# Value products with exchanged operands in 21 units of a fused attention and feed-forward kernel

## The chip, the cores and the metric

The kernel runs on one core of a Trainium2 chip. A core has engines that work side by side, each through its own instructions in order: TensorE (PE; PEld are its weight loads), VectorE (DVE), ScalarE (ACT), GpSimd (POOL) and SyncE (SP, which here only issues transfers). SBUF is the working memory, PSUM the one in which TensorE leaves its products; both have 128 partitions. The metric is the device time of one execution in microseconds (us). TensorE's clock can be throttled; the profile has a row for what was granted.

## The reference

Two parts, one behind the other, computed here in bf16 operands with f32 sums. `P` is an 8x8 matrix per head that mixes the 8 blocks of 96 tokens.

```python
B, H, S, D = 4, 8, 768, 64            # 8 blocks of 96 tokens
P = sinkhorn(sort_net)                # five rounds of exp and normalising, per head 8x8
k_sorted, v_sorted = P @ k_blocks, P @ v_blocks
scores = q_block @ k_sorted_block.T / sqrt(D)          # 96x96 per head and block
attn = exp(scores - max(scores)); attn = attn / (sum(attn) + 1e-9)
x = attn @ v_sorted_block             # then (tokens, heads*64): 3072 x 512
h = x @ w_in                          # 512 x 2048
out = (h * cos(h)) @ w_out            # 2048 x 512
```

## The kernel before

The 3072 tokens are cut into 8 chunks `n` of 384 tokens, half a batch each, and a chunk into four units `u` of one block of 96 tokens with all 8 heads (4 pairs `h2` of two, `hp`). A chunk's attention is followed by its feed-forward layer, and while one chunk's layer runs the next chunk's attention is fed in between. The order is written out by hand: `PLAN` (L18 on) is a list of some 800 steps, and each step issues its instructions to the engines' queues in that order. An engine does its instructions strictly in this order, so a step that waits holds up everything behind it on the same engine.

The steps that matter here, for unit `n u`:

- S or T: scores on TensorE. M (L1362) and X (L1376, L1372): VectorE takes the maximum per row and subtracts it. E (L1380): ScalarE's exponential gives the weights, in bf16, query by row.
- TP (L1407) and TE, or TD (a transposing transfer): the weights turned to `pT`, 96 key rows by 8 heads x 96 queries.
- AV (L1431): eight products on TensorE, one per head, with `pT` as the stationary operand and the mixed values (64 columns and a column of ones) as the moving one. The output has the queries in its partitions, and 65 columns per head: 64 sums and, in the last, the sum of the weights.
- N (L1447, L1448): VectorE takes the reciprocal of the 8 sums per query and multiplies the 512 sums with them, into `xn` in bf16.
- XP (L1470) and XE (L1071 on ScalarE, L1073 on VectorE): four turns of `xn` on TensorE, into PSUM, and a copy to `xT`, the layer's input with features in its partitions. In 11 of the 32 units a transposing transfer (XD) does both; these units are not touched by the change. In chunks 0 to 2 the token order inside a unit is permuted (queries are loaded four rows at a time), and the turns set it right by multiplying with a permuted identity, `order` (L1154).
- U (L1500), C (L1506) and G (L1512): the layer's first product, its cosine on ScalarE and the multiply on VectorE; U4 (L1523), C4, G4 (L1536) are the same for chunk 0, by halves of 192 tokens, so that its first half needs units 0 and 1 alone. D (L1545), O and W: the second product, the copy out of PSUM and the store.
- QP and QE turn later queries and copy them; k and v mixing (kp, ks, kg, v0, vb, vg and their copies, kse and vbe among them) run in between.

PSUM is shared out as three tiles of two banks (`big`, "B" in the plan) and two of one bank (`acc`, "c"). AV, U, U4 and most scores use `big`: a tile comes free when its last reader is done, and the third next `big` step waits for it. In chunk 0 AV is preceded by a few idle products (`keep_warm`).

Of the kernel before, what the change touches and what calls it, by code (L numbers as in the profile page):

```python
# [65 lines left out]
kxp 0  # L66
TP 0 1 c
X 0 2
AV 0 0
z_turned 1  # L70
TE 0 1 V
E 0 2 0
TP 0 3 c
Lk 1
Lv 1
N 0 0
AV 0 1
N 0 1
pk2
TE 0 3 A  # L80
TP 0 2 B
TE 0 2 A
QP 1 1 c
QE 1 1 0 V
XP 0 0 B
XE 0 0 A
XP 0 1 c
z_vperm
XE 0 1 V
AV 0 2  # L90
N 0 2
AV 0 3
z_turned 0
U4 0 0 0
U4 0 0 1
C4 0 0
p_pads
N 0 3
U4 0 1 0
QE 1 1 1 V  # L100
XP 0 3 c
G4 0 0
U4 0 1 1
C4 0 1
XP 0 2 c
XE 0 2 V
U4 0 3 0
U4 0 3 1
G4 0 1
XE 0 3 A  # L110
U4 1 2 0
U4 1 3 0
C4 0 3
# [57 lines left out]
TP 1 3 c  # L171
TE 1 3 A
TP 1 0 B
AV 1 2
X 1 1
W 0 1
TE 1 0 A
W 0 0
D 0 2 1
D 0 2 2  # L180
AV 1 3
E 1 1 1
TP 1 1 c
AV 1 0
TE 1 1 A
N 1 2
XP 1 2 B
XE 1 2 A
N 1 3
D 0 2 3  # L190
AV 1 1
O 0 2 t A
W 0 2
ks 3 B
kse 3 A
N 1 0
XP 1 0 B
XE 1 0 A
ks 2 c
kse 2 A  # L200
N 1 1
XP 1 3 c
XE 1 3 V
ks 1 B
XP 1 1 B
XE 1 1 V
# [97 lines left out]
D 1 1 0  # L304
D 1 1 1
D 1 1 2
AV 2 0
Lpv 3 6
Lpv 4 6
Lpv 5 6  # L310
N 2 0
kg 4 c
kge 4 A
Lq 4
# [2 lines left out]
E 2 3 2  # L317
D 1 1 3
M 3 0
AV 2 1  # L320
N 2 1
kg 3 B
O 1 1 o A
X 3 0
D 1 2 0
kge 3 A
TP 2 3 c
AV 2 2
N 2 2
XP 2 1 B  # L330
XE 2 1 V
D 1 2 1
TE 2 3 A
AV 2 3
kg 5 B
N 2 3
XP 2 2 B
XP 2 0 c
E 3 0 0
D 1 2 2  # L340
XP 2 3 B
XE 2 2 V
W 1 1
XE 2 3 A
D 1 2 3
XE 2 0 V
kge 5 A
U 2 0
C 2 0
# [77 lines left out]
D 2 1 1  # L427
M 4 0
X 4 0
AV 3 1  # L430
N 3 1
vge 0 8 A
D 2 2 0
E 4 0 1
D 2 1 2
D 2 1 3
AV 3 2
vg 4 8 B
AV 3 3
N 3 3  # L440
D 2 2 1
D 2 2 2
S 4 1 c 0
N 3 2
XP 3 1 B
vge 4 8 A
XE 3 1 V
XP 3 3 B
vg 6 8 B
XE 3 3 V  # L450
O 2 1 o A
vge 6 8 A
XP 3 2 B
XE 3 2 V
D 2 2 3
O 2 2 o V
W 2 1
# [87 lines left out]
TD 5 0  # L545
E 5 1 0
TD 5 1
AV 4 2
N 4 2
D 3 2 0  # L550
AV 4 3
D 3 2 1
D 3 2 2
XP 4 2 B
QD 6
N 4 3
XP 4 3 B
hq 0
XE 4 2 A
D 3 2 3  # L560
Lq 7
XE 4 3 V
U 4 1 1
C 4 1
O 3 2 v V
# [63 lines left out]
XD 5 2  # L629
D 4 1 3  # L630
O 4 1 v A
AV 5 3
D 4 2 0
N 5 3
D 4 2 1
XP 5 3 B
XE 5 3 A
E 6 1 1
D 4 2 2
D 4 2 3  # L640
# [66 lines left out]
E 7 0 1  # L707
D 5 1 3
O 5 1 v A
AV 6 3  # L710
N 6 3
TD 7 0
T 7 2 B
D 5 2 1
# [1 line left out]
X 7 1  # L716
E 7 1 2
TD 7 1
XP 6 3 B
XE 6 3 A  # L720
W 5 0
M 7 2
D 5 2 2
# [48 lines left out]
D 6 1 0  # L772
D 6 1 1
D 6 1 2
AV 7 2
D 6 1 3
O 6 1 v V
D 6 2 0
AV 7 3
N 7 2  # L780
N 7 3
D 6 2 1
XP 7 2 B
D 6 2 2
XD 7 1
XP 7 3 B
D 6 2 3
XE 7 3 A
XE 7 2 V
U 7 0  # L790
W 6 0
W 6 1
# [40 lines left out]
def kernel(  # L833
# [36 lines left out]
    const = ctx.enter_context(tc.tile_pool(name="const", bufs=1))  # L870
# [18 lines left out]
    ident = const.tile([128, 128], BF16, name="ident")  # L889
# [19 lines left out]
    vS = {}  # L909
    QR, NQ = 4, 3  # L910
# [115 lines left out]
    def picks(t, batches):  # L1026
        nc.gpsimd.memset(t[:], 0.0)
        for z, b in enumerate(batches):
            picked(t, z, b)
# [5 lines left out]
        nc.gpsimd.memset(vS[g][:, :, D:D + 1], 1.0)  # L1035

    picks(pick, (1, 0, 1))
    order = const.tile([blk, blk], BF16, name="order")
    warm = const.tile([128, 128], BF16, name="warm")
    nc.vector.memset(warm[:], 0.0)  # L1040
    half_pi = const.tile([128, 1], FP32, name="half_pi")
    nc.vector.memset(half_pi[:], math.pi / 2)
    nc.vector.memset(vperm[:, CD:], 0.0)
    nc.vector.memset(kbuf[:64, :32 * D], 0.0)
    nc.vector.memset(q_turned[0][:, :, QW:], 0.0)
# [21 lines left out]
    V, A = nc.vector, nc.scalar  # L1067
# [31 lines left out]
    E, Q = E_eps[:, :, :nb], Q_eps[:, :nb]  # L1099
# [209 lines left out]
    s_t, pT, xn_t, xT, gt, out_ps, kept = {}, {}, {}, {}, {}, {}, {}  # L1309
# [102 lines left out]
    def v_at(g, b2, hp, h2, i):  # L1412
        return (b2 * 2 + hp) * NB + h2 * nb + i

    def AV(n, u, pool=big, tag="big"):
# [11 lines left out]
        for hp in range(2):  # L1427
            for h2 in range(H2):
# [5 lines left out]
                    vS[g][:, v_at(g, b2, hp, h2, ih * IC + u), :D + 1],  # L1434
                    start=True, stop=True)

    def N(n, u):
        r = small.tile([blk, 2, H2], FP32, name="r", tag="r")
        xn = xn_t[n, u] = small.tile([blk, H2, 2, D], BF16, name="xn", tag="xn")
        parts = [slice(0, 2)] if ("a", n, u) in ps else [slice(0, 1), slice(1, 2)]  # L1440
        for e in parts:
            if len(parts) == 1:
                a = ps.pop(("a", n, u))[:blk, :, :H2 * (D + 1)]
            else:
                a = ps.pop(("a", n, u, e.start))[:blk, :H2 * (D + 1)].unsqueeze(1)
            avv = a.rearrange("p e (h w) -> p e h w", w=D + 1)
            nc.vector.reciprocal(r[:, e].unsqueeze(3), avv[:, :, :, D:])  # L1447
            nc.vector.tensor_tensor(  # L1448
                xn.rearrange("p h e d -> p e h d")[:, e], avv[:, :, :, :D],
                r[:, e].to_broadcast([blk, e.stop - e.start, H2, D]), op=ALU.mult)  # L1450
# [11 lines left out]
    def XP(n, u, pool, tag, to=None):  # L1462
        us = range(u, (u if to is None else to) + 1)
        o = kept_tile(("x", n, u), pool, tag, [128, KC, len(us), blk], BF16, "xps")

        turn = order[:] if n < NQ else ident[:blk, :blk]
        for i, z in enumerate(us):
            xn = xn_t.pop((n, z))
            for h2 in range(H2):
                nc.tensor.transpose(  # L1470
                    o[:, h2, i], xn[:, h2].rearrange("p e d -> p (e d)"), turn)
# [204 lines left out]
```

## Time and profile before

| what | value |
|---|---|
| median of three timed runs | 235.09 us (235.08 to 235.13) |
| span of the profiled execution | 233.6 us |
| instructions | 5709 |
| AV on TensorE | 32 units of 8 products, 193 ns each from issue to end |
| N on VectorE | 32 reciprocals of 198 ns, 32 multiplies of 687 ns |
| XP on TensorE | 84 turns, 205 ns each from issue to end |
| XE | 12 copies on VectorE of 348 ns, 9 on ScalarE of 475 ns |

The profile is of one execution, taken by the hardware profiler. The profiled execution has no timed figure of its own beside its span; the span runs from its first to its last instruction and lies 1.5 us under the timed median. Busy time is what an engine's instructions cover. Products on TensorE are pipelined: the duration of one product is longer than the distance to the next, so the cost of a group is read from the chain of work, which shows distances, and not from durations. A row of the timeline gives the start, the length, the engine, the line, the operation with output and input, and how many instructions it merges; what stands in brackets is the engine's idle time before it, and what ended it. A row of the groups by line gives busy time and mean duration behind the bar, and then the idle time ahead of the group.

### The profile page before, as it was taken

How to read it: one execution, taken by the hardware profiler on the slowest of the kernel's cores; microseconds unless marked ns; L12 is line 12 of the kernel's file. 1: busy time of each engine (PE TensorE's matmuls, PEld its weight loads, DVE VectorE, ACT ScalarE, POOL GpSimd, SP SyncE). 2: the span in 40 equal slices, each digit the busy share in tenths (PEclk: the TensorE clock that was granted, in tenths of full speed). 3: DMA queues.
4: the chain of work that ended last, by engine and by line, in shares of the span. 5: the costliest groups of instructions: out<-in, count | busy, mean ns of one | idle time of the engine just before them, and what ended most of it. 6: DMA issues, size and time to landing. Idle time of an engine off the chain costs nothing.

```text
span 233.6 us, 5709 instructions
## 1 busy us (share of the span) xinstructions
PE 224.9 (96%) x2358; PEld 148.6 (64%) x2378; DVE 173.8 (74%) x290; ACT 149.9 (64%) x199; POOL 93.7 (40%) x117
## 2 busy tenths in 40 slices
PE   8799999999999999989999999999999999999994
PEld 5379899567665666645666558645655596456553
DVE  5759986897889777886778977898587779445630
ACT  3367965668869768783789746764766376536411
POOL 7689996598970186963508001700000000000000
PEclk9999999999999999999999999999999999999999
DMA  5999999994899899997989659954943360250103
GB/s 74 222 194 206 205 207 227 198 209 144 105 108 156 186 163 157 101 208 144 137 161 81 90 94 167 196 85 78 149 157 68 66 189 3 50 141 3 46 0 135
DMA packets 66842, 31.01 MB, mean 133 GB/s; under 512 B 55553, under 2 KB 62337, under 8 KB 66561
## 3 DMA queue, kind: packets, MB, share of 16 engines
q0 software_dynamic: 24048, 13.64, 42.8%
q1 hardware_dynamic: 42480, 16.83, 34.3%
q8 instruction: 18, 0.29, 0.5%
q10 hardware_dynamic: 288, 0.20, 0.3%
q14 instruction: 8, 0.06, 0.1%
HBM read 27.27 MB, written 6.29 MB: 144 GB/s over the span
## 4 chain that ended last, share of the span: by engine, by line
PE 77%; DMA 7%; ACT 4%; POOL 4%; DVE 3%; issue 2%; SPq 1%; POOLq 0%; ACTq 0%
PE o L1545 28%; PE h L1500 27%; PE h L1523 5%; DMA kv<-in_v_dram 3%; PE av L1431 3%; POOL vperm L993 2%; DMA kTs<-kTs 2%; PE vs L1258 2%; PE sc L1321 2%; PE o L1640 2%; DMA pT<-p_buf 1%; PE pps L1407 1%; PE vs L1293 1%; PE xps L1470 1%; PE ks L1202 1%
## 5 line engine op out<-in xcount | busy, mean ns | idle before, releaser
L1545 PE MATMUL o<-w_out_t,gg 128*128 128x512 bf16 x349 | 85.1, 379 | 1.1 <-issue 0.2
L1500 PE MATMUL h<-xT,w_in_t 128*128 128x384 bf16 (+1 forms) x524 | 78.4, 303 | 0.0
L1512 DVE TENSOR_TENSOR gg<-c,h 128x768 bf16<-128x768 f32 x56 | 52.8, 948 | 21.2 <-ACT c L1506 21.1
L1506 ACT ACTIVATE c<-h,half_pi 128x768 f32<-128x768 f32 x56 | 50.4, 901 | 20.0 <-PE h L1500 18.8
L1500 PEld LDWEIGHTS <-w_in_t 128*128 128x128 bf16 x524 | 47.7, 98 | 22.2 <-DVE xT L1073 0.4
L1545 PEld LDWEIGHTS <-gg 128*128 128x128 bf16 x368 | 33.1, 98 | 32.9 <-DVE gg L1512 0.6
L1380 ACT ACTIVATE p_buf<-s 96x768 bf16<-96x768 f32 x32 | 26.4, 841 | 12.7 <-DVE s L1376 10.3
L1362 DVE TENSOR_REDUCE mx<-sc 96x8 f32<-96x768 f32 (+1 forms) x41 | 31.5, 771 | 0.7 <-PE sc L1321 0.4
L993 POOL COPY vperm<-kv 64x1536 bf16<-64x1536 bf16 (+1 forms) x10 | 28.1, 2848 | 3.7 <-DMA kv<-in_v_dram 3.7
L1376 DVE TENSOR_TENSOR s<-sc,mx 96x384 f32<-96x384 f32 (+1 forms) x33 | 24.2, 733 | 1.3
L1448 DVE TENSOR_TENSOR xn<-av,r 96x512 bf16<-96x512 f32 x32 | 22.0, 687 | 1.1
L943 POOL DMA_DIRECT2D kv<-in_q_dram x24 | 16.0, 680 | 0.8 <-issue 0.5
L1071 ACT CAST kTs<-ks 128x512 bf16<-128x512 f32 (+1 forms) x18 | 11.0, 635 | 3.6 <-PE ks L1202 3.6
L943 POOL DMA_DIRECT2D q_mem<-in_q_dram x16 | 10.7, 684 | 3.4 <-DMA kv<-in_v_dram 2.9
L1447 DVE RECIPROCAL r<-av 96x8 f32<-96x8 f32 x32 | 6.3, 198 | 7.3 <-PE av L1431 7.1
L1523 PE MATMUL h<-xT,w_in_t 128*128 128x192 bf16 x128 | 11.4, 246 | 0.0
L1060 PE MATMUL idle<-warm 128*128 128x512 bf16 (+4 forms) x46 | 9.0, 364 | 2.3 <-ACT q_turned L1143 1.2
L1060 PEld LDWEIGHTS <-warm 128*128 128x128 bf16 x106 | 7.7, 111 | 5.5 <-issue 2.8
L1071 ACT COPY kv<-o 128x512 f32<-128x512 f32 (+2 forms) x10 | 5.3, 528 | 9.1 <-PE o L1545 6.5
L1071 ACT COPY xT<-xps 128x384 bf16<-128x384 bf16 x9 | 4.3, 475 | 10.3 <-PE xps L1470 10.3
L1523 PEld LDWEIGHTS <-w_in_t 128*128 128x128 bf16 x128 | 10.4, 98 | 0.1
L1568 POOL CAST held<-q_turned 96x1 f32<-96x1 bf16 x2 | 0.4, 182 | 24.4 <-DVE gg L1512 16.9
(120 smaller groups left out, 276.5 us busy)
## 6 DMA issues: line engine op xcount, KB each, us to landing
out_dram<-kv SPq DMA_DIRECT2D x12, 256.0 KB, 2.4
out_dram<-o_s SPq DMA_DIRECT2D x10, 256.0 KB, 3.0
w_in_t<-in_moe_w_in_dram POOLq DMA_DIRECT2D x4, 512.0 KB, 12.4
w_out_t<-in_moe_w_out_dram POOLq DMA_DIRECT2D x4, 512.0 KB, 12.7
kv<-in_k_dram POOLq DMA_DIRECT2D x2, 768.0 KB, 10.2
kv<-in_v_dram POOLq DMA_DIRECT2D x2, 768.0 KB, 13.6
pair<-in_k_dram POOLq DMA_DIRECT2D x2, 768.0 KB, 10.9
kv<-in_v_dram POOLq DMA_DIRECT2D x6, 256.0 KB, 6.1
```

The source lines that it names most:

```text
L943: nc.gpsimd.dma_start(out=q_heads[:, i, :, e], in_=src[:, ih * IC + i, :, e])
L993: nc.gpsimd.tensor_copy(dst, src)
L1071: eng.copy(dst, src)
L1362: nc.vector.reduce_max(mx[:], s_view(n, u, hp), axis=AX.XY if n < 2 else AX.X)
L1376: nc.vector.tensor_tensor(s, sc, mx.to_broadcast(list(s.shape)), op=ALU.subtract)
L1380: nc.scalar.activation(p[:, :, :blk], s_t.pop((n, u)).rearrange("p e h c -> p (e h) c"), AF.Exp, scale=scale)
L1448: nc.vector.tensor_tensor(xn.rearrange("p h e d -> p e h d")[:, e], avv[:, :, :, :D], r[:, e].to_broadcast([blk, e.stop - e.start, H2, D]) ...
L1500: nc.tensor.matmul(o[:, f2, x * w:(x + 1) * w], w_in_t[:, kk, f * 128:(f + 1) * 128], xT[n][:, kk, x * w:(x + 1) * w], start=(kk == 0), st ...
L1506: nc.scalar.activation(c[:], ps["h", n, fp][:, :, :TC], AF.Sin, bias=half_pi[:, 0:1])
L1512: nc.vector.tensor_tensor(gt[n, fp // 2][:, f:f + 2], ps.pop(("c", n, fp))[:], ps.pop(("h", n, fp))[:, :, :TC], op=ALU.mult)
L1523: nc.tensor.matmul(o[:, part, f2 * w:(f2 + 1) * w], w_in_t[:, kk, f * 128:(f + 1) * 128], xT[0][:, kk, h * w:(h + 1) * w], start=(kk == 0) ...
L1545: nc.tensor.matmul(out_ps[n, ts][:], gt[n, q][:, f % 4, ts * 128:(ts + 1) * 128], w_out_t[:, f, :], start=(f == 0), stop=(f == FC - 1))
```

## The change

In 21 units the steps AV, N, XP and XE are replaced by two, AT and NT. The 21 are all units of chunks 0, 1 and 2, units 1 to 3 of chunk 3, units 2 and 3 of chunks 4 and 7, and unit 3 of chunks 5 and 6. In the plan AT and NT stand where AV and N stood; XP and XE go.

AT exchanges the operands of the value products: the mixed values (64 columns) are stationary and the turned weights move, 96 columns per head. Heads with `e` = 0 fill output partitions 0 to 63, those with `e` = 1 partitions 64 to 127, so the output is `xT` before its normalisation. The sums come out of two products of a block of ones (`unit`, 96x64) with 4 heads x 96 columns of weights each; every output partition of a half holds the sum that belongs to its column. NT takes the reciprocal of all these 128x384 sums, writes it as f32 over the unit's `pT`, and multiplies the 128x384 products with it, straight into `xT`. In chunks 0 to 2 the multiply's access pattern sets the token order right, and `order` goes.

```diff
@@ the plan, chunks 1 and 7 as examples @@
-AV 1 0
+AT 1 0
 TE 1 1 A
-N 1 2
-XP 1 2 B
-XE 1 2 A
-N 1 3
+NT 1 2
+NT 1 3
 D 0 2 3
...
-AV 7 3
-N 7 2
-N 7 3
+AT 7 3
+NT 7 2
+NT 7 3
 D 6 2 1
-XP 7 2 B
 D 6 2 2
 XD 7 1
-XP 7 3 B
 D 6 2 3
-XE 7 3 A
-XE 7 2 V
 U 7 0
...
@@ the start @@
-    order = const.tile([blk, blk], BF16, name="order")
...
+    unit = const.tile([blk, D], BF16, name="unit")
+    nc.vector.memset(unit[:], 1.0)
...
-            A.copy(
-                order.rearrange("k (p r) -> k p r", r=QR),
-                ident[:blk, :blk].rearrange("k (r p) -> k p r", r=QR))
...
@@ the new steps @@
+    def AT(n, u, pool=big, tag="big"):
+        g, b2, ih = where(n)
+        a = kept_tile(("at", n, u), pool, tag, [128, 2, 512], FP32, "at")
+        pt = pT[n, u].rearrange("p a c -> p (a c)")
+        if n == 0:
+            keep_warm(1, a[:, 1], 256)
+        for h2 in range(H2):
+            for e in range(2):
+                x = (e * H2 + h2) * blk
+                nc.tensor.matmul(
+                    a[e * D:(e + 1) * D, 0, h2 * blk:(h2 + 1) * blk],
+                    vS[g][:, v_at(g, b2, e, h2, ih * IC + u), :D], pt[:blk, x:x + blk],
+                    start=True, stop=True)
+        for e in range(2):
+            nc.tensor.matmul(
+                a[e * D:(e + 1) * D, 1, :H2 * blk], unit[:],
+                pt[:blk, e * H2 * blk:(e + 1) * H2 * blk], start=True, stop=True)
+
+    def NT(n, u):
+        a = ps.pop(("at", n, u))
+        over_sum = pT.pop((n, u)).rearrange("p a c -> p (a c)").bitcast(FP32)
+        nc.vector.reciprocal(over_sum, a[:, 1, :H2 * blk])
+        x = x_to(n)[:, :, u * blk:(u + 1) * blk]
+        num, den = a[:, 0, :H2 * blk], over_sum
+        if n < NQ:
+            x = x.rearrange("p k (c r) -> p k r c", r=QR)
+            num, den = [t.rearrange("p (k r c) -> p k r c", k=KC, r=QR) for t in (num, den)]
+        else:
+            num, den = [t.rearrange("p (k c) -> p k c", k=KC) for t in (num, den)]
+        nc.vector.tensor_tensor(x, num, den, op=ALU.mult)
```

More of the change, by code (lines that the diff above doesn't have):

```diff
@@ L68 @@
 X 0 2
-AV 0 0
+AT 0 0
 z_turned 1
@@ L75 @@
 Lv 1
-N 0 0
-AV 0 1
-N 0 1
+NT 0 0
+AT 0 1
+NT 0 1
 pk2
@@ L84 @@
 QE 1 1 0 V
-XP 0 0 B
-XE 0 0 A
-XP 0 1 c
 z_vperm
[L89 to L92, printed above, removed]
+AT 0 2
+NT 0 2
+AT 0 3
 z_turned 0
@@ L97 @@
 p_pads
-N 0 3
+NT 0 3
 U4 0 1 0
 QE 1 1 1 V
-XP 0 3 c
 G4 0 0
@@ L104 @@
 C4 0 1
-XP 0 2 c
-XE 0 2 V
 U4 0 3 0
@@ L109 @@
 G4 0 1
-XE 0 3 A
 U4 1 2 0
@@ L173 @@
 TP 1 0 B
-AV 1 2
+AT 1 2
 X 1 1
@@ L180 @@
 D 0 2 2
-AV 1 3
+AT 1 3
 E 1 1 1
 TP 1 1 c
-AV 1 0
+AT 1 0
 TE 1 1 A
-N 1 2
-XP 1 2 B
-XE 1 2 A
-N 1 3
+NT 1 2
+NT 1 3
 D 0 2 3
-AV 1 1
+AT 1 1
 O 0 2 t A
@@ L195 @@
 kse 3 A
-N 1 0
-XP 1 0 B
-XE 1 0 A
+NT 1 0
 ks 2 c
 kse 2 A
-N 1 1
-XP 1 3 c
-XE 1 3 V
+NT 1 1
 ks 1 B
-XP 1 1 B
-XE 1 1 V
 ks 0 B
@@ L306 @@
 D 1 1 2
-AV 2 0
+AT 2 0
 Lpv 3 6
@@ L310 @@
 Lpv 5 6
-N 2 0
+NT 2 0
 kg 4 c
@@ L319 @@
 M 3 0
-AV 2 1
-N 2 1
+AT 2 1
+NT 2 1
 kg 3 B
@@ L327 @@
 TP 2 3 c
[L328 to L331, printed above, removed]
+AT 2 2
+NT 2 2
 D 1 2 1
 TE 2 3 A
-AV 2 3
+AT 2 3
 kg 5 B
-N 2 3
-XP 2 2 B
-XP 2 0 c
+NT 2 3
 E 3 0 0
 D 1 2 2
-XP 2 3 B
-XE 2 2 V
 W 1 1
-XE 2 3 A
 D 1 2 3
-XE 2 0 V
 kge 5 A
@@ L429 @@
 X 4 0
-AV 3 1
-N 3 1
+AT 3 1
+NT 3 1
 vge 0 8 A
@@ L436 @@
 D 2 1 3
-AV 3 2
+AT 3 2
 vg 4 8 B
-AV 3 3
-N 3 3
+AT 3 3
+NT 3 3
 D 2 2 1
@@ L443 @@
 S 4 1 c 0
-N 3 2
-XP 3 1 B
+NT 3 2
 vge 4 8 A
-XE 3 1 V
-XP 3 3 B
 vg 6 8 B
-XE 3 3 V
 O 2 1 o A
 vge 6 8 A
-XP 3 2 B
-XE 3 2 V
 D 2 2 3
@@ L547 @@
 TD 5 1
-AV 4 2
-N 4 2
+AT 4 2
+NT 4 2
 D 3 2 0
-AV 4 3
+AT 4 3
 D 3 2 1
 D 3 2 2
-XP 4 2 B
 QD 6
-N 4 3
-XP 4 3 B
+NT 4 3
 hq 0
-XE 4 2 A
 D 3 2 3
 Lq 7
-XE 4 3 V
 U 4 1 1
@@ L631 @@
 O 4 1 v A
-AV 5 3
+AT 5 3
 D 4 2 0
-N 5 3
+NT 5 3
 D 4 2 1
-XP 5 3 B
-XE 5 3 A
 E 6 1 1
@@ L709 @@
 O 5 1 v A
-AV 6 3
-N 6 3
+AT 6 3
+NT 6 3
 TD 7 0
@@ L718 @@
 TD 7 1
-XP 6 3 B
-XE 6 3 A
 W 5 0
@@ L774 @@
 D 6 1 2
-AV 7 2
+AT 7 2
 D 6 1 3
@@ L1464, in XP @@
         o = kept_tile(("x", n, u), pool, tag, [128, KC, len(us), blk], BF16, "xps")
-        turn = order[:] if n < NQ else ident[:blk, :blk]
         for i, z in enumerate(us):
@@ L1470, in XP @@
                 nc.tensor.transpose(
-                    o[:, h2, i], xn[:, h2].rearrange("p e d -> p (e d)"), turn)
+                    o[:, h2, i], xn[:, h2].rearrange("p e d -> p (e d)"), ident[:blk, :blk])
     def XE(n, u, eng, to=None):
@@ L1620 @@
         kp=kp, kpe=kpe, kxp=kxp, ks=ks, kse=kse, kg=kg, kge=kge, kswap=kswap, v0=v0, v0e=v0e,
-        vb=vb, vbe=vbe, vg=vg, vge=vge, S=S, M=M, X=X, E=E, TD=TD, TP=TP, TE=TE, AV=AV, N=N,
+        vb=vb, vbe=vbe, vg=vg, vge=vge, S=S, M=M, X=X, E=E, TD=TD, TP=TP, TE=TE, AV=AV, N=N, AT=AT, NT=NT,
         XD=XD, XP=XP, XE=XE, QP=QP, QE=QE, QD=QD, U=U, C=C, G=G, U4=U4, C4=C4, G4=G4, D=D4,
```

## The prediction

> **What bounds the kernel now.** I read the page's head first, then the chain of work that ended last, then the stages.
>
> ```profile
> span 233.6 us, 5709 instructions
> ...
> PE 224.9 (96%) x2358; PEld 148.6 (64%) x2378; DVE 173.8 (74%) x290; ACT 149.9 (64%) x199; POOL 93.7 (40%) x117
> ...
> PEclk9999999999999999999999999999999999999999
> ...
> PE 77%; DMA 7%; ACT 4%; POOL 4%; DVE 3%; issue 2%; SPq 1%; POOLq 0%; ACTq 0%
> ```
>
> TensorE is busy 96% of the span at an undisturbed clock, and the chain runs through it for 77%; the detours over other engines are short. So TensorE time counts nearly one for one, and every moment in which TensorE must wait for VectorE is new time. VectorE's 74% looks like slack, but it is a mean over two kinds of stage. The busy times by stage, cut where value products and normalisation (N) stand against the layer's stages, say more:
>
> ```profile
> 24.00:33.00 9.00, 8.82 (x161) 8.37 (x161) 7.96 (x17) 7.53 (x11) 8.64 (x15) 1.00 1.28 206
> ...
> 74.00:86.00 12.00, 11.89 (x132) 7.52 (x128) 9.73 (x18) 8.50 (x15) 4.90 (x9) 1.00 0.90 154
> ...
> 209.00:221.00 12.00, 11.95 (x80) 7.48 (x79) 6.23 (x7) 7.47 (x8) 0.00 (x0) 1.00 0.07 24
> ```
>
> After the stretch and its length the columns are TensorE, its weight loads, VectorE, ScalarE and POOL. In the first stage with N (24 to 33) VectorE has 1.0 us left of 9; at 74 to 86 it has 2.3 of 12; only the layer stages have much (209 to 221: 5.8 of 12). What the change does on VectorE falls on the tight ones.
>
> **The change part by part: TensorE.** A unit is 96 tokens with 8 heads. Per unit, 8 value products (AV) and, later, 4 turns (XP) go; 8 products of 96 columns into half the output partitions, in alternate halves, and 2 products of 384 columns with the block of ones come (AT).
>
> ```profile
> 27.43 0.53 PE qps L1082 x16
> ...
> 28.53 0.26 PE av L1431 x8
> ...
> 57.88 0.83 PE qps L1082 x32
> ...
> 59.05 1.30 PE h L1500 x8
> ...
> 112.38 0.34 PE xps L1470 x8
> ```
>
> AV is 0.26 us and four turns half of 0.34, so 0.43 us go. The query turns (qps) have AT's shape, 96 rows, 64 columns of weights, 96 moving columns, 64 partitions out: 0.83/32 to 0.53/16, 26 to 33 ns each, under the 42 ns of a full-width turn, so the halves run partly beside each other. Eight take 0.21 to 0.26 us. A product of 384 columns takes 1.30/8 = 0.16 us; two take 0.16 us side by side, 0.33 in turn. AT is thus 0.37 to 0.59 us, a change of -0.06 to +0.16 per unit, over 21 units -1.3 to +3.4 us. I take 0, near the side-by-side end, where the query turns point; both ends stay for the range.
>
> The Trainium skill (TensorEngine Tiling (Array Packing), Restrictions and Key Properties) speaks against this part: half-width products lose the fast weight load, and changing the tiling mode drains TensorE. Charged with one product of 384 columns per unit for the drain, an estimate, it would add 21 x 0.16 = 3.4 us to the sum. The rows above show no such price: the 16 query turns stand between full-width work and still average under a full-width turn.
>
> **VectorE.** N is a reciprocal of 8 numbers per row and a multiply of 512; NT is a reciprocal of 384 and a multiply of 384.
>
> ```profile
> L1448 DVE TENSOR_TENSOR xn<-av,r 96x512 bf16<-96x512 f32 x32 | 22.0, 687 | 1.1
> L1376 DVE TENSOR_TENSOR s<-sc,mx 96x768 f32<-96x768 f32 x15 | 14.3, 951 | 0.8
> L1376 DVE TENSOR_TENSOR s<-sc,mx 96x384 f32<-96x384 f32 x18 | 9.9, 552 | 0.5
> L1447 DVE RECIPROCAL r<-av 96x8 f32<-96x8 f32 x32 | 6.3, 198 | 7.3 <-PE av L1431 7.1
> L1073 DVE COPY xT<-xps 128x384 bf16<-128x384 bf16 x12 | 4.0, 348 | 1.4 <-PE xps L1470 1.4
> L1073 DVE COPY kv<-o 128x512 f32<-128x512 f32 x4 | 2.8, 688 | 4.0 <-PE o L1545 4.0
> L1124 DVE RECIPROCAL over<-sums 32x8 f32<-32x8 f32 x5 | 1.0, 191 | 0.2
> L1119 DVE TENSOR_TENSOR less<-P,top 32x64 f32<-32x64 f32 x1 | 0.2, 214 | 0.0
> L1118 DVE TENSOR_REDUCE top<-P 32x8 f32<-32x64 f32 x1 | 0.2, 207 | 0.2 <-DMA P<-in_sort_net_dram 0.2
> ```
>
> The multiply is priced by its neighbour of the same length, 0.55 us. The reciprocal decides everything, and no long one is in the trace. The two subtractions (L1376) give VectorE's pace, (951 - 552)/384 = 1.04 ns per element. With it the fixed part of an operation is 214 - 67 = 147 ns (subtraction of 64), 207 - 67 = 140 (maximum of 64), 688 - 532 = 156 (copy of 512). A reciprocal of only 8 takes 191 ns: as long as about 45 elements of another operation. Either its fixed part is 183 ns, larger than any of these, or its elements are slow: (191 - 147)/8 = 5.5 ns and (191 - 140)/8 = 6.4 ns each, 4.4 ns with the copy's fixed part. For 384, 191 + 376 x the price: 0.58 us at 1.04 ns (lower end), 1.85 us at 4.4, 2.6 us at 6.4. I take 6 ns, between the two rows that lie nearest in size and memory: **2.45 us**. The upper end is below, among the rivals.
>
> ```profile
> 205.83 0.19 DVE L1447 RECIPROCAL r<-av 96x8 f32<-96x8 f32 x1
> ...
> 206.66 0.19 DVE L1447 RECIPROCAL r<-av 96x8 f32<-96x8 f32 x1
> ```
>
> From one N's start to the next's is 0.83 us, 0.05 less than the two durations. NT occupies VectorE 2.45 + 0.55 - 0.05 = **2.95 us**, 2.12 more than N. Twenty-one of them add 44.5 us; the 12 copies of turned tokens that leave VectorE give back 12 x 0.35 = 4.2. That is two thirds of VectorE's 59.8 us of idle time, most of which lies in the layer stages and not where NT stands. The 9 copies that leave ScalarE, the dropped ordering block and the added block of ones at the start count nothing: ScalarE is not late in these stages, and the block of ones is a small fill ahead of work that waits for a load.
>
> **Stage by stage**, each time from the first changed unit's N (its reciprocal's row) to the first TensorE product that needs the finished layer input (U or U4). Queued behind NT on VectorE are query copies, score maxima and subtractions (M, X) and the layer's multiplies (G, G4), and TensorE waits for their buffers too; in stages without NT, TensorE has no idle time in which to recover.
>
> ```profile
> 25.96 0.19 DVE L1447 RECIPROCAL r<-av 96x8 f32<-96x8 f32 x1
> 31.46 0.95 DVE L1536 TENSOR_TENSOR gg<-c,h 128x768 bf16<-128x768 f32 x1 [0.28 <-ACT c L1529]
> 32.15 5.31 PE h L1523 x64
> 52.45 0.19 DVE L1447 RECIPROCAL r<-av 96x8 f32<-96x8 f32 x1
> 59.69 2.05 DVE L1073 COPY q_turned<-qps 64x768 bf16<-64x768 bf16 x4
> 61.77 0.95 DVE L1512 TENSOR_TENSOR gg<-c,h 128x768 bf16<-128x768 f32 x1
> 79.54 0.20 DVE L1447 RECIPROCAL r<-av 96x8 f32<-96x8 f32 x1 [1.46 <-PE av L1431]
> 86.49 1.46 PE L1500 MATMUL h<-xT,w_in_t 128*128 128x384 bf16 x8
> 107.98 0.19 DVE L1447 RECIPROCAL r<-av 96x8 f32<-96x8 f32 x1
> 114.20 1.30 PE h L1500 x8
> 136.34 0.19 DVE L1447 RECIPROCAL r<-av 96x8 f32<-96x8 f32 x1
> 139.54 2.71 PE h L1500 x28
> 159.83 0.19 DVE L1447 RECIPROCAL r<-av 96x8 f32<-96x8 f32 x1
> 163.30 2.60 PE h L1500 x16
> 183.55 0.20 DVE L1447 RECIPROCAL r<-av 96x8 f32<-96x8 f32 x1 [0.59 <-PE av L1431]
> 186.83 7.90 PE h L1500 x88
> 209.24 7.82 PE h L1500 x56
> ```
>
> - n = 0, four units: 25.96 + 4 x 2.95 + two query copies of 2.05/4 = 38.8 for the first G4, which stood at 31.46. The fourth U4 tile needs that G4's buffer, free at 39.7; it started 16 products into the row of 32.15, at 33.5. **+6.2 us.**
> - n = 1, four: 52.45 + 11.8 = 64.25 before U 1 0, which started at 59.05: +5.2; the first G, behind two copies of 512 elements (0.64 each with the overlap) and the four query copies (2.05), moves from 61.77 to 67.5, +5.7. **+5.5.**
> - n = 2, four, with M and X of the next chunk between (0.95 us each less the overlap): 79.54 + 11.8 + 1.8 = 93.1 against 86.49. **+6.6.**
> - n = 3, three: 107.98 + 8.85 = 116.85 against 114.20. **+2.65.**
> - n = 4, two: 136.34 + 5.9 = 142.25 against 139.54. **+2.7.**
> - n = 5 and 6, one each: 162.8 against 163.30, 186.5 against 186.83. **0**, with 0.5 and 0.3 us of cover left.
> - n = 7, two: 205.83 + 5.9 = 211.73 against 209.24. **+2.5.**
>
> The sum is +26.1 us. The profile's span of 233.6 us lies 1.5 under the timed median of 235.09, and I carry that over: 235.1 + 26.1 = **261 us**.
>
> **The rivals.**
>
> *The long reciprocal runs at VectorE's pace* and its 183 ns fixed part is its own. Then it takes 0.58 us, NT 1.08 us, 0.25 more than N; four units cost 1.0 us, most of which the removed copies (0.35 us each) and the waits for turns give back, and gates with cover do not move. TensorE's -1.3 to +3.4 us remain, with up to 0.7 in n = 0: 233.5 to 239 us, 234.5 if the halves run side by side, below before by the shorter TensorE work. It decides below about 0.8 us per reciprocal, where four units' extra (4 x 0.47) is about what copies and gaps of one stage return. For it: a fixed part that is longer by 40 ns would explain both short rows as well. Against it: three other operations agree on 140 to 156. Chance 0.14, not slower in 0.09 of it.
>
> *Eight clocks per element.* Eight times 1.04 is 8.3 ns, so the reciprocal takes 191 + 376 x 8.3 = 3.3 us, 0.86 more than I take; 19 units stand ahead of a moved gate (4, 4, 4, 3, 2 and 2), which adds 16.4, and the covers at n = 5 and 6 are overrun by about 0.9 together: 279 us. Against it: the fixed part would be only 125 ns. The Trainium skill (VectorE: DVE Perf Modes, First, the fixed hardware budget) says that the reciprocal is an iterated divide with a repeat count of 8, which would give this rival. By that rule the forecast would be these 279 us; the short rows here lean to fewer clocks, and no run here yet shows a long one. Chance of the rival 0.2.
>
> *A middling reciprocal*, 4.4 ns and 1.85 us: 0.6 less at 19 units, 11.4 us less: 250 us. Chance 0.16.
>
> *Waits of TensorE that cool its clock*: the clock row is full because no gap is long, and now gaps of 3 us appear. No row shows the price; at half pace for as long as each of some six gaps it would be up to 9 us. I leave it out of the forecast and in the range.
>
> **How the numbers follow.** My forecast, 5.5 to 6.4 ns, has 0.5: 258 to 265 us. The middling case and the eight clocks widen this to 247 to 283, which leaves out the fast reciprocal and a little more. What the measurement tells from no change is about 0.2%, 0.5 us: faster 0.06, within 0.03, slower 0.91, nearly all of the fast reciprocal's chance being split between the three.
>
> **What would show it.** The reciprocal's row: 128x384 at about 2450 ns (580 or 3300 for the rivals). VectorE's busy time: 173.8 + 40, so over 210 us. TensorE's busy time near 225 us with gaps before U and U4 of n = 0 to 4 and 7, ended by VectorE's multiply in NT, and none at n = 5 and 6. Two products with the ones 160 or 330 ns apart. I am wrong if the reciprocal is short, or if TensorE finds other work in the waits, which its fixed order of instructions speaks against.

## The result and the profile after

The changed kernel takes 280.03 us (279.62 to 281.01, four runs) against 235.11 us before (235.08 to 235.23): a ratio of 1.192, 95% interval 1.190 to 1.194. The head of the page after, in the order of the head before:

```profile
span 278.4 us, 5613 instructions
...
PE 241.5 (87%) x2315; PEld 151.5 (54%) x2336; DVE 220.4 (79%) x279; ACT 146.0 (52%) x189; POOL 93.5 (34%) x117
...
PEclk9999959999589999799997999799999999997999
...
PE 58%; DVE 30%; issue 4%; ACT 4%; POOL 1%; another core or an unknown queue 1%; DVEq 0%; POOLq 0%; ACTq 0%
```

VectorE has gone from 3% to 30% of the chain that ended last, and from 173.8 to 220.4 us of work. TensorE has 16.6 us more of busy time (241.5 against 224.9). The change gives it no such amount of new work; but its clock row, full before, now has seven digits below 9. What VectorE does longer stands in the groups by line (L1414 and L1422 are the two lines of NT):

```profile
L1414 DVE RECIPROCAL pT<-at 128x384 f32<-128x384 f32 x16 | 40.6, 2537 | 2.4 <-PE at L1407 2.4
L1422 DVE TENSOR_TENSOR xT<-at,pT 128x384 bf16<-128x384 f32 x16 | 14.4, 901 | 0.5
...
L1422 DVE TENSOR_TENSOR xT<-at,vperm 128x384 bf16<-128x384 f32 x4 | 2.2, 558 | 0.1
```

The reciprocal takes 2.54 us, where 2.45 had been taken. The multiply takes 0.56 us where it writes in natural order; the 16 of the second row are 12 in the permuted order of chunks 0 to 2 and 4 plain ones, so a permuted one takes (16 x 901 - 4 x 558)/12 = 1015 ns. That difference had not been in the sum.

The times at which the first layer products stand, from the chain of work of the kernel after (start, length, what):

```profile
40.44 5.81 PE h L1509 x64
...
75.03 2.72 PE h L1486 x8
...
113.15 2.74 PE h L1486 x8
...
146.11 2.16 PE h L1486 x8
...
176.34 4.23 PE h L1486 x28
...
201.96 2.60 PE h L1486 x16
...
234.71 2.60 PE h L1486 x16
...
252.19 9.68 PE h L1486 x56
```

The first row, in chunk 0, stood at 32.15 before and lies 8.3 us later. Set against the rows before (59.05, 86.49, 114.20, 139.54, 163.30, 209.24), those of chunks 1 to 5 and 7 lie 16.0, 26.7, 31.9, 36.8, 38.7 and 43.0 us later: the loss grows from chunk to chunk. (The row of 234.71 stands inside chunk 6; the same products before are shown below.) The second thing to see is the lengths: 8 products that took 1.30 us before take 2.72, 2.74 and 2.16. The busy times by stage show why, for the wait before chunk 2 and the stretch after it, and the same for chunk 3 (stretch, its length, TensorE, its weight loads, VectorE, ScalarE, POOL, granted clock, busy share of the transfer engines, GB/s):

```profile
108.30:113.10 4.80, 0.06 (x1) 0.00 (x0) 4.73 (x5) 0.55 (x1) 4.80 (x2) 0.95 0.86 65
113.10:115.90 2.80, 2.75 (x11) 1.40 (x12) 0.51 (x1) 0.00 (x0) 2.80 (x2) 0.50 0.44 120
143.00:146.10 3.10, 0.07 (x1) 0.00 (x0) 3.07 (x3) 1.54 (x2) 0.00 (x0) 1.00 0.87 75
146.10:149.50 3.40, 3.39 (x16) 1.95 (x17) 1.83 (x4) 1.19 (x2) 0.00 (x0) 0.60 0.72 119
```

While TensorE waits for VectorE (4.73 of 4.80 us busy) the clock is still granted for nearly all of the wait; in the stretch behind it the clock is half, and the first products pay. Cut into windows of 0.1 us, the half clock in this kernel runs from 34.1 to 40.9, 68.2 to 78.5, 112.6 to 116.0, 146.8 to 150.2, 177.5 to 180.9 and 252.6 to 256.0 us. In chunks 0 and 1 (the first two) it begins inside the stage, ahead of the row shown for the chunk.

### The profile page after: what moved, and what is told of

It is laid out like the page before. It is cut to its first block, busy times and chain, and to the rows that moved or that the text cites. A ratio compares the mean times of both kernels' runs of the same rounds, so it can differ in the third digit from the quotient of the medians.

```text
span 278.4 us, 5613 instructions
## 1 busy us (share of the span) xinstructions
PE 241.5 (87%) x2315; PEld 151.5 (54%) x2336; DVE 220.4 (79%) x279; ACT 146.0 (52%) x189; POOL 93.5 (34%) x117
## 4 chain that ended last, share of the span: by engine, by line
PE 58%; DVE 30%; issue 4%; ACT 4%; POOL 1%; another core or an unknown queue 1%; DVEq 0%; POOLq 0%; ACTq 0%
PE h L1486 25%; PE o L1531 17%; DVE pT L1414 13%; DVE xT L1422 3%; PE h L1509 3%; DVE vperm L1414 3%; DVE mx L1318 2%; DVE gg L1498 2%; DVE s L1332 2%; PE ks L1158 2%; PE vs L1214 2%; PE sc L1277 1%; PE o L1626 1%; ACT c L1492 1%; DVE kv L1414 1%
## 5 line engine op out<-in xcount | busy, mean ns | idle before, releaser
L1486 PE MATMUL h<-xT,w_in_t 128*128 128x384 bf16 (+1 forms) x524 | 86.3, 322 | 15.5 <-DVE xT L1422 14.7
L1492 ACT ACTIVATE c<-h,half_pi 128x768 f32<-128x768 f32 x56 | 50.3, 900 | 55.8 <-PE h L1486 54.1
L1486 PEld LDWEIGHTS <-w_in_t 128*128 128x128 bf16 x524 | 50.5, 103 | 42.8 <-DVE xT L1422 13.0
L1414 DVE RECIPROCAL pT<-at 128x384 f32<-128x384 f32 x16 | 40.6, 2537 | 2.4 <-PE at L1407 2.4
L1509 PE MATMUL h<-xT,w_in_t 128*128 128x192 bf16 x128 | 13.3, 267 | 5.5 <-DVE xT L1422 5.5
L1509 PEld LDWEIGHTS <-w_in_t 128*128 128x128 bf16 x128 | 11.7, 106 | 6.7 <-issue 6.3
L1422 DVE TENSOR_TENSOR xT<-at,pT 128x384 bf16<-128x384 f32 x16 | 14.4, 901 | 0.5
L1515 ACT ACTIVATE c<-h,half_pi 128x768 f32<-128x768 f32 x8 | 7.1, 900 | 13.8 <-PE h L1509 12.7
L1019 PE MATMUL idle<-warm 128*128 128x512 bf16 (+4 forms) x46 | 9.7, 385 | 2.1 <-DVE half_pi L999 1.0
L901 POOL DMA_DIRECT2D q_mem<-in_q_dram x16 | 10.7, 691 | 1.5 <-DMA kv<-in_v_dram 1.1
L1414 DVE RECIPROCAL vperm<-at 128x384 f32<-128x384 f32 x4 | 10.2, 2552 | 0.7 <-PE at L1407 0.7
## 6 DMA issues: line engine op xcount, KB each, us to landing
out_dram<-kv SPq DMA_DIRECT2D x12, 256.0 KB, 2.6
out_dram<-o_s SPq DMA_DIRECT2D x10, 256.0 KB, 2.3
kv<-in_v_dram POOLq DMA_DIRECT2D x6, 256.0 KB, 5.7
```

The costliest lines, as they stand in the source:

```text
L901: nc.gpsimd.dma_start(out=q_heads[:, i, :, e], in_=src[:, ih * IC + i, :, e])
L1414: nc.vector.reciprocal(over_sum, a[:, 1, :H2 * blk])
L1422: nc.vector.tensor_tensor(x, num, den, op=ALU.mult)
L1486: nc.tensor.matmul(o[:, f2, x * w:(x + 1) * w], w_in_t[:, kk, f * 128:(f + 1) * 128], xT[n][:, kk, x * w:(x + 1) * w], start=(kk == 0), st ...
L1492: nc.scalar.activation(c[:], ps["h", n, fp][:, :, :TC], AF.Sin, bias=half_pi[:, 0:1])
L1509: nc.tensor.matmul(o[:, part, f2 * w:(f2 + 1) * w], w_in_t[:, kk, f * 128:(f + 1) * 128], xT[0][:, kk, h * w:(h + 1) * w], start=(kk == 0) ...
```

## The experiments

Theory: the length of the reciprocal makes nearly all of the time, through TensorE's waits, and the half clock, the permuted multiply and a smaller loss on TensorE make the part above the forecast. Rivals: the exchange on TensorE or the longer hold of PSUM tiles makes the time; the losses of a stage are partly won back; the slow first products have another reason.

**The reciprocal shortened**, x1_short:

```diff
-        nc.vector.reciprocal(over_sum, a[:, 1, :H2 * blk])
+        nc.vector.tensor_scalar(over_sum, a[:, 1, :H2 * blk], 1e-4, None, op0=ALU.mult)
```

> NT's reciprocal of 384 sums is replaced by a multiplication of the sums with 0.0001 (same input, same output, same length), so the output is not normalised. Theory (the length of the reciprocal makes the time): VectorE needs about 0.55 us in place of 2.54, a unit in chunks 0 to 2 about 1.4 us in place of 3.4 and in the later ones 0.95 in place of 2.95, nearly all of TensorE's waits and its half clock behind them go: 236 to 242 us. Rival (the exchanged products or the longer hold of PSUM tiles make the time): at least 255 us.

Measured: 238.12 us, a ratio to before of 1.014 (1.012 to 1.016). The operation in the reciprocal's place, in the groups by line of this kernel:

```profile
L1414 DVE TENSOR_SCALAR pT<-at 128x384 f32<-128x384 f32 x16 | 8.9, 558 | 3.6 <-PE at L1407 3.6
```

With 1.98 us less per unit on VectorE, 41.9 of the 44.9 us are gone and the mean granted clock is back from 0.945 to 0.997. AT and the permuted multiply are still there, so neither makes the time. What x1_short does not separate is the hold of AT's PSUM tile: the tile comes free with NT's multiply, so it too is held 1.98 us less. Both are effects of the same long reciprocal, and the waits of the changed kernel's trace tell them apart in part: of TensorE's waits that end with NT's multiply, 14.7 us stand ahead of U, which needs the finished layer input, and 6.7 us ahead of `ks` (4.3) and AT (2.4), which read nothing that NT writes and so wait for the tile.

**The token order of the multiply**, x2_plain and x4_read. First in natural order:

```diff
-        if n < NQ:
+        if False:
             x = x.rearrange("p k (c r) -> p k r c", r=QR)
```

> NT's multiply writes the tokens of chunks 0 to 2 in natural order, not in the permuted one, so these tokens stand in the wrong rows of the output. Theory (the 1.01 us of the permuted multiply against 0.56 of the plain one lies on the path in chunks 0 to 2): 12 x 0.46 = 5.5 us less, about 274.5 us. Rival (there the wait is set by something else): over 278 us.

then in the order of the output, with the steps on the side of the inputs:

```diff
-            x = x.rearrange("p k (c r) -> p k r c", r=QR)
-            num, den = [t.rearrange("p (k r c) -> p k r c", k=KC, r=QR) for t in (num, den)]
+            x = x.rearrange("p k (c r) -> p k c r", r=QR)
+            num, den = [t.rearrange("p (k r c) -> p k c r", k=KC, r=QR) for t in (num, den)]
```

> The same computation, but the multiply of chunks 0 to 2 goes through the tokens in the order of its output: the bf16 output is written densely and the two f32 inputs are read in steps of 24 elements. Theory A (the scattered 2-byte writes cost the 0.46 us): the multiply takes 0.56 us and the kernel 274.5 us. Theory B (any order with steps costs it, on whichever side): 1.0 us and 280 us.

Measured: x2_plain 275.64 us (ratio to before 1.172, 1.166 to 1.178), 4.4 under the changed kernel; x4_read 276.86 us (1.179, 1.174 to 1.184), 3.2 under it. The multiplies in the groups by line, of x2_plain and then of x4_read:

```profile
L1422 DVE TENSOR_TENSOR xT<-at,pT 128x384 bf16<-128x384 f32 x16 | 8.9, 558 | 0.5
```

```profile
L1422 DVE TENSOR_TENSOR xT<-at,pT 128x384 bf16<-128x384 f32 x16 | 11.8, 741 | 0.5
```

In natural order all take 558 ns. With strided reads the 12 take (16 x 741 - 4 x 558)/12 = 802 ns. So neither theory of x4_read holds as written: steps cost on both sides, 0.46 us where bf16 is written in steps and 0.24 us where f32 is read in steps. That rests on the durations. The totals are too scattered for it (273.7 to 276.6 us in the four runs of x2_plain, 275.9 to 278.5 in those of x4_read): they separate neither the two kernels from each other nor the 4.4 us that x2_plain saved from the 5.5 expected.

**The clock kept up**, x3_warm:

```diff
         o = kept_tile(("h", n, fp), big, "big", [128, 2, 512], FP32, "h")
+        for _ in range({(2, 0): 15, (3, 0): 13, (4, 1): 12, (7, 0): 12}.get((n, fp), 0)):
+            nc.tensor.matmul(o[:, 0], warm[:], warm[:, :1].to_broadcast([128, 512]), start=True, stop=True)
```

> Ahead of the first layer product of chunks 2, 3, 4 and 7 stand 15, 13, 12 and 12 products of zeros, 512 columns each, in that product's own PSUM tile: they run while TensorE waits for NT. Theory (the products behind a long wait are slow because the clock is halved after the wait): the clock stays full there, and the slow products lose 1.4, 1.6, 1.5 and 1.9 us: about 273.5 us. Rival (they are slow for another reason, or the clock falls all the same): 280 us or more.

Measured: 274.71 us, 1.168 (1.166 to 1.171) of before, 5.3 us under the changed kernel with 52 products more. Chunk 3's stretch after the wait, and chunk 2's first products in the timeline:

```profile
146.00:148.50 2.50, 2.50 (x19) 1.59 (x19) 1.63 (x4) 1.03 (x2) 0.00 (x0) 1.00 0.38 116
```

```profile
114.42 1.46 PE L1488 MATMUL h<-xT,w_in_t 128*128 128x384 bf16 x8 [1.52 <-DVE xT L1422]
```

The clock is full where it was 0.60, and eight products are back at 1.46 us with the last one's tail. Chunk 2's first product still starts only when NT is done; the half clock behind the waits went, which is what was to be told apart. The four stages are worth more than the total says. In the profiled execution chunk 2's first product comes 1.3 us later than in the changed kernel (114.42 against 113.15), and chunks 0 and 1, which the edit does not touch, fell otherwise on the half clock (32.5 to 42.7 and 70.0 to 80.2 us). Against that the first products of chunks 3, 4 and 5 and the last tile gain 1.4, 1.7, 1.6 and 1.7 us, one after the other: 6.4 us in all, as the expectation added up.

Whether a wait is followed by half clock is not a matter of its length alone. The first products of chunk 4, in the changed kernel and then in x2_plain, stand behind waits of the same 2.79 us:

```profile
176.34 4.23 PE L1486 MATMUL h<-xT,w_in_t 128*128 128x384 bf16 x28 [2.79 <-DVE xT L1422]
```

```profile
173.13 2.79 PE L1486 MATMUL h<-xT,w_in_t 128*128 128x384 bf16 x28 [2.79 <-DVE xT L1422]
```

In the first the clock is half from 177.5 to 180.9, in the second it is full, and 28 products differ by 1.44 us. The stretches at half clock have a common measure. By the trace's records of the clock those of the changed kernel, x2_plain, x3_warm, x4_read and x6_chunk2, but for the last one at the kernel's end, are 3.41, 6.83 or 10.24 us long, once, twice or three times 3.413; and the six starts in the changed kernel lie 34.13, 44.38, 34.13, 30.72 and 75.09 us apart, 10, 13, 10, 9 and 22 times 3.413. Where the waits fall against these steps of 3.413 us differs from execution to execution. That this decides whether a wait costs clock fits these rows, but no run tested it by itself.

**What the exchange costs alone**, x5_short_plain (x1_short and x2_plain together):

> Both long terms of VectorE are left out: the reciprocal is replaced by a multiplication with 0.0001, so the output is not normalised, and chunks 0 to 2 are written in natural token order. What is left of the change is the exchange itself: AT in place of AV and turns on TensorE, one pass over the sums and one multiply in place of N and the copies. Theory (the exchange alone is worth nothing on TensorE: AT 0.46 us per unit against 0.43, and VectorE near what it was): 235.0 to 236.5 us. Rival (the exchange costs, by drains or slow half-width loads): 238 us or more. Other rival (it gains): under 234 us.

Measured: 237.34 us, 1.0095 (1.0081 to 1.0109) of before, 2.1 us above it, between the two expectations. The timeline of TensorE in this kernel, around one AT:

```profile
81.46 1.03 PE L1531 MATMUL o<-w_out_t,gg 128*128 128x512 bf16 x4
82.42 0.36 PE L1402 MATMUL at<-pT,vS 96*64 96x96 bf16 x8
82.61 0.33 PE L1407 MATMUL at<-pT,unit 96*64 96x384 bf16 x2
82.87 0.40 PE L1158 MATMUL ks<-bd,pair 128*128 128x128 bf16 x4
83.11 1.03 PE L1531 MATMUL o<-w_out_t,gg 128*128 128x512 bf16 x4
83.97 0.52 PE L1363 MATMUL pps<-ident,p_buf 96*96 96x96 bf16 x8
```

Four products of 512 columns need 0.86 us to the next start when turns of full width follow (83.11 to 83.97), and 0.96 when AT follows (81.46 to 82.42): 0.10 us of nothing ahead of AT. Before, four such products ahead of AV needed 0.87 (105.63 to 106.50), so AV had no such gap; the scores with 64 rows of weights had it before too (0.97 ahead of them, 100.04 to 101.01). Inside AT the eight products need 0.19 us, 24 ns each on average, and from the first product with the ones to the next full-width work are 0.26 us, which is 0.16 for two side by side and again 0.10. AT costs 0.10 + 0.19 + 0.26 = 0.55 us per unit against 0.43 for AV and turns. Two kernels tested that reading.

**One operation for NT, and no sums**, x10_one_op, and x11_no_sums without the two products as well:

```diff
     def NT(n, u):
         a = ps.pop(("at", n, u))
...
-        nc.vector.reciprocal(over_sum, a[:, 1, :H2 * blk])
+        pT.pop((n, u))
         x = x_to(n)[:, :, u * blk:(u + 1) * blk]
...
-        nc.vector.tensor_tensor(x, num, den, op=ALU.mult)
+        nc.vector.tensor_scalar(
+            x, a[:, 0, :H2 * blk].rearrange("p (k c) -> p k c", k=KC), 0.01, None, op0=ALU.mult)
```

> NT is one operation: the products times 0.01 straight into the layer input, in natural token order; the reciprocal and the multiply with it are left out, so the output is not normalised, and the products with the ones still run. VectorE has 0.55 us per unit where the kernel before has 0.83 and a copy. Theory (what remains of the exchange, 2.1 us with x5_short_plain, is TensorE's: 0.10 us of nothing ahead of AT and 0.10 behind it, where before has none, 0.55 us per unit against 0.43, 21 x 0.12 = 2.5): 236.8 to 237.6 us. Rival (it is VectorE's two operations per unit): 235.5 us or less.

> As x10_one_op, but the two products with the ones are left out of AT as well. Theory (two products of 384 columns side by side, 0.16 us per unit, go; the 0.10 us ahead and behind stay): 21 x 0.16 = 3.4 us under x10_one_op, about 233.8 us. If the two run one after the other (0.33 us): 7 us less. If the empty time belongs to the products with the ones and not to the change of width: 21 x 0.26 = 5.5 us less.

Measured: x10_one_op 237.03 us, 1.008 (1.007 to 1.009) of before. VectorE has 9.7 us less to do than before (164.1 against 173.8), and the 1.8 us remain: more work on VectorE cannot be their reason, and the 0.12 us per unit on TensorE are enough for them. x11_no_sums missed by far: 239.26 us, 1.016 (1.014 to 1.019), slower with less work. Its chain, after x10_one_op's, at the first product of chunk 2:

```profile
88.26 1.30 PE h L1480 x8
```

```profile
86.50 1.30 PE h L1476 x8
...
100.14 6.81 DMA kTs<-kTs
...
106.99 0.48 PE sc L1304 x7
107.47 1.82 PE o L1521 x4
```

Up to there it is as expected: 1.76 us over 12 units, 0.15 per unit, are saved, and it stands where the kernel before stood (86.49). Then TensorE comes to the first scores with chunk 3's keys while the transfer that swaps their halves is under way. It waits 2.49 us there (0.71 before, none in x10_one_op), and the clock halves behind that wait as well: four products of 512 columns take 1.82 us. TensorE arrives only 0.2 us earlier than before; the transfer lands 1.6 us later (106.95 against 105.33) and takes 6.81 us in place of 5.56. Why it is longer stays open. The half clock is not the whole loss either: two of the five runs had a mean clock of 0.998, as x10_one_op had, and still took 238.2 and 238.3 us. The reading of 0.10 us on either side is borne out by x10_one_op and by the stretch up to chunk 2; the total of x11_no_sums tells nothing of it.

**Single stages**, x6_chunk2 and x7_chunks56: the kernel before with the edit of the changed one in these chunks alone (the block of ones stands in the memory of a table that is only used at the start):

```diff
@@ x6_chunk2; the same for 5 3 and 6 3 in x7_chunks56 @@
-AV 2 0
+AT 2 0
...
-N 2 0
+NT 2 0
...
-XP 2 1 B
-XE 2 1 V
```

> The kernel before, with AT and NT in the four units of chunk 2 alone. Theory (each stage's loss is made where it stands and nothing of it is won back): the first layer product of chunk 2 comes 8 us later and the products behind it lose 1.5 us to the half clock, 244 to 246 us. Rival (a loss in one stage is made good in the next ones, which then have slack): under 241 us.

> The kernel before, with AT and NT in the last unit of chunk 5 and of chunk 6 alone. The prediction's account: both waits are covered, 235.1 us. The changed kernel's trace: nothing at chunk 5, but at chunk 6 the subtraction behind NT is late for ScalarE's exponential and the load of its table, 1.1 us more, 236.3 us. Rival (2 x 2.1 us of VectorE count in full): 239 us.

x6_chunk2 measured 245.75 us, 1.0445 (1.042 to 1.047) of before. Its chain:

```profile
95.31 2.74 PE h L1526 x8
...
101.24 1.30 PE h L1526 x8
...
124.66 1.30 PE h L1526 x8
...
236.84 3.55 PE o L1666 x48
```

The third group of eight in the kernel before, from its timeline, and the last tile from its chain:

```profile
89.71 1.46 PE L1500 MATMUL h<-xT,w_in_t 128*128 128x384 bf16 x8
```

```profile
226.57 3.55 PE o L1640 x48
```

The first product of chunk 2 comes 95.31 - 86.49 = 8.8 us late; at the third group the half clock has made it 11.5. At chunk 3's first product (114.20 before) it is 10.5 and at the last tile 10.3. So 1.2 us are won back, 0.7 of them where the kernel before waited for the swap of keys, and the rest is carried through 112 us. x7_chunks56 measured 236.54 us, 1.0056 (1.004 to 1.007), 1.3 more than before, and its chain in chunk 6 names the way:

```profile
183.13 2.57 DVE vperm L1457
...
186.19 0.95 DVE s L1375
...
187.17 0.84 ACT p_buf L1379
...
188.03 1.28 ACT L1536
...
189.33 0.91 ACT c L1536
```

TensorE has its layer input in time. But the next chunk's subtraction stands behind NT, ScalarE's exponential behind it, and the load of the cosine's table behind that: the first cosine starts at 189.33. The same in the kernel before, from ScalarE's timeline, and the later products of chunk 6 from its chain:

```profile
188.19 0.90 ACT L1506 ACTIVATE c<-h,half_pi 128x768 f32<-128x768 f32 x1 [0.30 <-PE h L1500]
```

```profile
194.90 2.60 PE h L1500 x16
```

The cosine is 1.1 us later with x7_chunks56. In the changed kernel these products stand at 234.71, 39.8 us later, where chunk 5's were 38.7: there too 1.1.

**The price of a reciprocal**, x9_lengths, all between SBUF tiles:

```diff
+    nc.vector.memset(ones_t[:], 2.0)
+    for w in (16, 64, 192, 384, 768):
+        nc.vector.reciprocal(over_t[:, :w], ones_t[:, :w])
+    with nc.allow_low_precision(reason="price of a bf16 output"):
+        nc.vector.reciprocal(over_t[:, :384].bitcast(BF16)[:, :384], ones_t[:, :384])
+    nc.vector.tensor_scalar(over_t[:, :384], ones_t[:, :384], 1e-4, None, op0=ALU.mult)
```

> The kernel before, with reciprocals of 16, 64, 192, 384 and 768 f32 numbers per partition, one of 384 with bf16 output, and a multiplication of 384 with 0.0001, all on VectorE between SBUF tiles ahead of the last tile's products. Only their rows count. Theory (a fixed 0.14 us and 6.25 ns per number, whatever the memory): 0.24, 0.54, 1.34, 2.54 and 4.94 us, and 2.54 with bf16 output. Rival (the price rises only in PSUM or at some length): 192 numbers or 384 in SBUF off this line by over 10%.

Only its rows are read; with them the kernel took 242.4 us in its one run. The rows in the groups by line:

```profile
L1639 DVE RECIPROCAL c<-c 128x768 f32<-128x768 f32 x1 | 5.0, 4953 | 0.0
...
L1641 DVE RECIPROCAL c<-c 128x384 bf16<-128x384 f32 x1 | 2.6, 2553 | 0.0
L1639 DVE RECIPROCAL c<-c 128x384 f32<-128x384 f32 x1 | 2.6, 2552 | 0.0
L1639 DVE RECIPROCAL c<-c 128x192 f32<-128x192 f32 x1 | 1.4, 1353 | 0.0
...
L1639 DVE RECIPROCAL c<-c 128x64 f32<-128x64 f32 x1 | 0.6, 553 | 0.0
L1642 DVE TENSOR_SCALAR c<-c 128x384 f32<-128x384 f32 x1 | 0.4, 361 | 0.0
```

(4953 - 2552)/384 = 6.25 ns per number, and 2552 - 384 x 6.25 = 152 ns fixed; 192 and 64 lie on that line (1352 and 552). PSUM or SBUF, f32 or bf16 out: no difference. Six of VectorE's steps of 1.04 ns go into one reciprocal. The Trainium skill (VectorE: DVE Perf Modes, First, the fixed hardware budget) has a repeat count of 8 for it; taken as eight steps per number the measurement differs, and decides.

## Why the prediction held, and where its terms were off

The direction, the mechanism and the range held: 280.0 us lies within 247 to 283, with TensorE waiting for NT at the gates named in chunks 1 to 4 and 7. The forecast of 261 us was 19 us short, and 258 to 265 was too narrow. That the range still held is in part luck: its upper part was drawn for a reciprocal of eight clocks, which did not come, and other terms filled it. The time is close to the 279 us of that rival, but not by its mechanism: the reciprocal takes 2.54 us, not 3.3.

From one chunk's first products to the next's the loss grew by 8.3, 7.7, 10.7, 5.2, 4.9, 1.9, 1.1 and 3.1 us, and by 1.9 more up to the end; the forecast had 6.2, 5.5, 6.6, 2.65, 2.7, 0, 0 and 2.5. (Half clock behind a chunk's first products counts toward the next chunk here.)

- *The reciprocal from rows of 8 numbers*: right, 6.25 ns per number, within the forecast's 5.5 to 6.4. The 0.09 us more are 19 x 0.09 = 1.7 us. The rival at VectorE's pace fell with the first row, and x1_short shows what it would have given, 238.1 us, in the 233.5 to 239 worked out for it.
- *The multiply "priced by its neighbour of the same length"*: too low in chunks 0 to 2, 1.01 for 0.56 us, because the neighbour writes f32 in order and this one scatters bf16. 12 x 0.46 = 5.5 us by the durations; x2_plain measured 4.4, with a scatter that does not exclude 5.5.
- *The clock, "left out of the forecast"*: this was the largest omission. Six stages have waits of TensorE and a stretch at half clock. x3_warm took 5.3 us of it back at four of them by its total, 6.4 by its rows; chunk 1's first eight products lose another 2.72 - 1.30 = 1.4 and chunk 0's 64 lose 0.5. That is 7.2 to 8.3 us, inside the "up to 9" of the range. The sign "TensorE's busy time near 225 us" failed with it: it is 241.5 us, where x1_short, at full clock, has 229.7.
- *TensorE's own work, taken as 0*: 0.55 us per unit for AT, inside the bounds of 0.37 to 0.59, but by another split. The two halves do run side by side; what costs is the entry into and the exit from the half-width products, 0.10 us each. The prediction said that the rows before "show no such price". They do:

```profile
32.15 5.31 PE h L1523 x64
...
37.76 2.09 PE h L1523 x24
39.84 0.49 PE qps L1082 x16
```

  64 products stand 0.083 us apart, so 24 need 1.99; the row of 2.09 that ends at the query turns holds 0.10 us of nothing. A mean over 16 products hid it. The Trainium skill (TensorEngine Tiling (Array Packing), Key Properties) says that a change of the tiling mode drains TensorE, and gives no time for it. The trace agrees as far as it goes: there are 0.10 us of nothing at each change, also ahead of the scores with 64 rows, which have the full output width, so the half width of the output is not needed for it. Over 21 units 0.12 us make 2.5; 1.8 were measured with x10_one_op, where a wait of 0.71 us for a transfer also went.
- *The gate at chunk 0, "the fourth U4 tile needs that G4's buffer"*: another wait came first. TensorE waited 2.64, 2.18 and 0.66 us ahead of the first three U4 tiles, each time until an NT was done and not for G4. The second of them:

```profile
37.06 2.72 PE L1509 MATMUL h<-xT,w_in_t 128*128 128x192 bf16 x16 [2.18 <-DVE xT L1422]
```

  The first needs the input of units 0 and 1; the next two, by the order of the plan, take the PSUM tiles that AT of units 2 and 3 held. The size came out all the same: the row of 64 ends 8.8 us later, and without 0.5 for the clock, 1.8 for the permuted multiplies and 0.4 for the longer reciprocals 6.1 are left, where 6.2 was forecast. That is luck, for the gate was the wrong one.
- *"0, with 0.3 us of cover left" at chunk 6*: the gate was the wrong one. The layer input was in time, the cosine was not: 1.1 us in the changed kernel, 1.3 with x7_chunks56. Chunk 5 was right.
- *Stage by stage, with "no idle time in which to recover"*: nearly right. x6_chunk2's first product is 8.8 us late, of which 6.6 had been forecast, 1.8 are the permuted multiplies and 0.4 the longer reciprocals; the half clock added 2.7 and 1.2 were won back.

26.1 + 1.7 + 5.5 + 2.5 + 1.1 = 36.9, and with 7.2 to 8.3 for the clock 44.1 to 45.2 us, against 44.9. The terms are not independent (shorter waits can also leave the clock alone), and each is good to some tenths at best, so the close agreement is not a proof of every term. That the exchange could be worth something with a short reciprocal is not shown either: x5_short_plain and x10_one_op, which do less than is needed, are both slower than before.

## What to carry to other kernels

Ask for the price per element of every operation that grows, not for the price of the instruction: a reciprocal of 8 numbers looks like any small operation, one of 384 takes 2.5 us, and the fixed part read off other operations of known length told them apart ahead of time. A transposed layout that turns 8 sums per row into a block of 384 copies has to pay for the copies on the engine that works on them. Price a wait of TensorE of some microseconds with the half clock that may follow it (1.4 to 1.7 us at each of four waits here), expect scatter between runs from it, and look for a late instruction on every engine that stands behind the moved one, not only at the gate that reads its result.

## What the runs showed of the hardware

- A reciprocal on VectorE takes 152 ns and 6.25 ns per number, from PSUM and SBUF alike, with f32 and bf16 output.
- Around waits of TensorE of 2.0 to 4.8 us (2.02 ahead of chunk 1's first product in x2_plain, 4.79 ahead of chunk 2's in the changed kernel) the clock was half for 3.41, 6.83 or 10.24 us. From chunk 2 on the fall came between 1.6 us ahead of the next product (x6_chunk2, 93.7 against 95.31) and 1.3 us behind it (chunk 3 of x2_plain, 144.2 against 142.91), and one wait of 2.79 us (chunk 4 of x2_plain) had none. With products of zeros in the wait the clock stayed at 1.00 in x3_warm.
- A multiply of 384 f32 numbers into bf16 takes 558 ns in order, 802 with both inputs read in steps of 24 elements, 1015 with the output written in steps of 4.
- Going into and out of products of half the output width leaves TensorE empty for 0.10 us each; inside, eight products of 96 columns stand 24 ns apart on average. Going into products with 64 rows of weights and full output width costs the same 0.10 us (100.04 to 101.01 in the kernel before).
- A multiplication of 384 f32 numbers with a constant takes 361 ns from SBUF and 558 from PSUM.
- A kernel with less work was slower (x11_no_sums, 239.3 us against 237.0 of x10_one_op): a transfer landed 1.6 us later than before, TensorE waited 2.49 us for it, and in the profiled execution the clock halved behind the wait.
